# A linear-attention block feeding a sparse causal-attention block: one recorded order for all instructions, PSUM in four pairs of banks

## The chip, the core and the metric

The kernel runs on one core of a Trainium2 chip. Five engines work at the same time, each through its own queue in the order in which its instructions were recorded: PE (matrix products), DVE (vector work), ACT (functions and copies), POOL (vector work that doesn't touch PSUM) and SP, which issues the transfers. The metric is the time of one launch on the device in microseconds (us). The three runs of the kernel before took 366.65, 371.04 and 371.76 us, a median of 371.04 us.

## The reference, cut to what matters

The input has 4 batches, 4 heads, 1088 tokens and 32 numbers per head. The first block squares two small projections of each key and query and runs attention without a softmax over them. The second block routes each token of the 128-wide result to 2 of 4 experts, each of which is a causal softmax attention over all 1088 tokens.

```python
phi(x): a = S1 @ x; b = S2 @ x            # 8 numbers each; all 64 products a_i*b_j
kv = sum over tokens of phi(k) * v;  z = sum of phi(k)
x  = (phi(q) @ kv) / (phi(q) @ z + 1e-6)  # 4 heads side by side: 128 numbers a token
logits = x @ w_gate;  the 2 best of 4 experts get softmax weights w
for each expert e:  scores = (x wq[e]) (x wk[e])^T / 8, causal
                    ye = softmax(scores) @ (x wv[e]) @ wo[e]
out = sum over the two chosen experts of w * ye
```

## The kernel before, in words

Both kernels fold `wq` and `wk` of an expert into one 128x128 matrix (`Mq`) and `wv` and `wo` into another (`Mo`). So the keys of every expert are the transposed activations `xT`, its values are `x` itself, and only the queries differ. A token has two slots, one for each chosen expert. A tile is 64 tokens with two slots: 128 rows. A batch has 17 tiles in three groups of 6, 6 and 5.

The work on a batch, with the lines of the profile:

- **Preparation** (`prepare`): load and transpose k and q; sketch them by small products (L478), copy the sketches out, multiply them to 64 features (L498); sum the features times v (L532, "sums"); transpose the query features (L546); multiply them by the sums (L567, `numer`); divide (L575 to L578); transpose to `xT` (L584); store `x` to memory and fetch it back in another layout (`xr`, tiles xra to xrc).
- **The choice**: gate logits (L628), comparisons on DVE (L649 to L659), weights of the two experts on POOL (L690 to L711). The masks of who chose whom go through memory to all partitions (L667, L671), as one byte per token.
- **Queries** of a group (L751): four products with `Mq`, two copied by ACT (L770) and all four picked by mask on DVE (L761, `copy_predicated`) into `qs`.
- **Scores** of a tile (L793) in chunks of at most 512 keys, one PSUM bank each. DVE takes a chunk out with the causal mask and a running minimum (L798), ACT exponentiates (L813), DVE inverts the sum (L818), POOL scales (L822), DVE transposes into `AT` (L827).
- **Values** of a group ("the V block", L847): products of 32 rows each, over all keys up to the group's end, into four banks. ACT and DVE read the sums out and mask them (L869, L879, L883), and POOL multiplies the outer two experts' part by their masks (L876).
- **Outputs** of a group (L903): four products with `Mo` for each 128 tokens, a copy (L911), stores (L917).

Eight PSUM banks: four single ones for everything that passes (`bank`), and a tile `V` of four banks, of which each group's V block takes one of two column ranges. During the first batch's preparation the four banks of `V` serve that work.

The order is made by the class `Plan`: each job has an engine, a length in us, a rank and the results and buffers that it needs. `Plan.order` plays the jobs against these lengths and takes, for each engine, the ready job of the lowest rank. The result is recorded once; on the chip each engine runs its list strictly in that order. Work on the next batch's preparation is ranked among the scores of this one, so that the small products of L478, L567, L584 and L628 stand between the large ones.

## Time and profile before

| | |
|---|---|
| median of three runs | 371.04 us |
| profiled execution, first to last instruction | 372.6 us |
| PE busy | 311.7 us (84%) |
| DVE busy | 209.0 us (56%) |
| ACT, POOL busy | 139.1 and 140.0 us |
| chain of waits that ended last | PE 53%, DVE 17%, POOL 9%, ACT 9%, issue 9% |
| moved by DMA | 24.37 MB |

The profiled execution has no time of its own beside the span; its 372.6 us stand 1.6 us above the median of the runs. Busy PE means that a product was somewhere in its pipeline, so 100% doesn't say that the array worked at its best rate. A stretch's granted clock of 1.00 is 2.4 GHz and 0.50 is 1.2 GHz; the column shows 1.00 before the first recorded change at 62 us, and there the lengths of the products have to be read. A wait is named after what released it last.

### The profile page before, as it was taken

What the parts mean: (1) busy time and instruction counts of PE and PEld (TensorE: products, weight loads), DVE (VectorE), ACT (ScalarE), POOL (GpSimd) and SP (SyncE); (2) the same over time, 40 slices, a digit from 0 to 9 for tenths busy, and PEclk for the clock granted to TensorE, in tenths of its full rate; (3) what the DMA queues carried; (4) which work ended last, traced back from release to release, by engine and by line L of the source; (5) the groups of instructions that cost most, each with busy time, mean ns of one, the idle gap of its engine ahead of it and who ended that gap; (6) DMA issues with size and microseconds to landing.
All of it is one profiled execution on the core that took longest, in us unless ns stands there. A gap on an engine that the chain in (4) does not pass through costs nothing.

```text
span 372.6 us, 11200 instructions
## 1 busy us (share of the span) xinstructions
PE 311.7 (84%) x4662; PEld 235.4 (63%) x4662; DVE 209.0 (56%) x611; ACT 139.1 (37%) x401; POOL 140.0 (38%) x236
## 2 busy tenths in 40 slices
PE   0876785799999689999996899899968999976953
PEld 0864642386658559866585598585746965846853
DVE  4540244636787671567976604659694279573330
ACT  1013233346452252564532525644424057162210
POOL 5100345445224626663246166542362044322220
PEclk9999998559999899999998999899987999996996
DMA  8931498374100307640103177001003390000000
GB/s 180 163 60 18 76 175 157 75 117 66 41 26 21 90 23 143 117 65 19 49 19 83 33 135 125 27 2 42 21 19 95 78 172 13 2 21 3 2 19 21
DMA packets 79038, 24.37 MB, mean 65 GB/s; under 512 B 51084, under 2 KB 77964, under 8 KB 78988
## 3 DMA queue, kind: packets, MB, share of 16 engines
q1 hardware_dynamic: 78972, 23.66, 32.4%
q8 instruction: 36, 0.59, 0.7%
q14 instruction: 14, 0.11, 0.1%
q10 hardware_dynamic: 16, 0.00, 0.0%
HBM read 19.18 MB, written 4.48 MB: 63 GB/s over the span
## 4 chain that ended last, share of the span: by engine, by line
PE 53%; DVE 17%; POOL 9%; ACT 9%; issue 9%; DMA 2%; SPq 0%; DVEq 0%; POOLq 0%; ACTq 0%
PE V L847 15%; PE bank L793 10%; PE bank L903 10%; DVE A L798 3%; POOL fp L498 3%; ACT A L813 3%; DVE AT L827 3%; PE V L478 2%; PE bank L532 2%; PE bank L751 2%; PE bank L567 2%; DVE agg L879 2%; POOL A L822 1%; DVE agg L883 1%; PE V L546 1%
## 5 line engine op out<-in xcount | busy, mean ns | idle before, releaser
L822 POOL TENSOR_SCALAR A<-A,rs,sh 128x192 f32<-128x192 f32 (+16 forms) x68 | 55.5, 821 | 97.7 <-DVE rs L818 92.4
L793 PE MATMUL bank<-xT,qs 128*128 128x320 f32 (+11 forms) x216 | 83.2, 507 | 4.5 <-DVE qs L761 2.5
L813 ACT ACTIVATE A<-A,mx 128x192 f32<-128x192 f32 (+16 forms) x68 | 52.4, 771 | 55.6 <-DVE mx L798 54.6
L827 DVE STREAM_TRANSPOSE AT<-A 128x192 f32<-128x192 f32 (+16 forms) x68 | 51.9, 768 | 15.8 <-POOL A L822 15.4
L793 PEld LDWEIGHTS bank<-xT,qs 128*128 128x128 f32 x216 | 38.5, 201 | 29.2 <-issue 9.3
L903 PE MATMUL bank<-Mo,agg 128*128 128x128 f32 (+1 forms) x288 | 43.2, 314 | 13.9 <-POOL g L703 8.7
L847 PE MATMUL V<-AT,xra 32*128 32x192 f32 (+5 forms) x1152 | 48.2, 316 | 6.0 <-DVE AT L827 6.0
L847 PEld LDWEIGHTS V<-AT,xra 32*128 32x128 f32 x1152 | 43.7, 195 | 14.2 <-DVE AT L827 9.7
L903 PEld LDWEIGHTS bank<-Mo,agg 128*128 128x128 f32 (+1 forms) x288 | 39.9, 217 | 19.8 <-POOL g L703 10.5
L751 PE MATMUL bank<-xT,Mq 128*128 128x384 f32 (+1 forms) x96 | 39.0, 529 | 4.8 <-DVE qs L761 4.0
L876 POOL TENSOR_TENSOR agg<-agg,uw 128x384 f32<-128x384 f32 (+1 forms) x24 | 22.4, 954 | 50.4 <-ACT uw L869 48.1
L798 DVE CUSTOM_DVE_ANT_0 A<-bank,mask 128x320 f32<-128x320 f32 (+11 forms) x68 | 33.9, 509 | 11.9 <-PE bank L793 11.4
L879 DVE TENSOR_TENSOR agg<-V,mb 128x384 f32<-128x384 f32 (+1 forms) x24 | 12.2, 529 | 44.6 <-PE V L847 37.5
L869 ACT COPY uw<-V 128x384 f32<-128x384 f32 (+1 forms) x24 | 9.9, 464 | 60.6 <-DVE agg L879 45.9
L751 PEld LDWEIGHTS bank<-xT,Mq 128*128 128x128 f32 x96 | 18.4, 208 | 19.2 <-DVE qs L761 8.1
L798 DVE CUSTOM_DVE_ANT_0 A<-bank,mask,mx 128x320 f32<-128x320 f32 (+7 forms) x40 | 23.9, 608 | 10.3 <-PE bank L793 8.5
L847 PE MATMUL V<-AT,xrb 32*128 32x160 f32 (+5 forms) x768 | 27.2, 290 | 0.0
L847 PEld LDWEIGHTS V<-AT,xrb 32*128 32x128 f32 x768 | 25.8, 185 | 1.3 <-issue 1.1
L761 DVE COPY_PREDICATED qs<-mb,bank 128x384 f32<-128x384 uint8 (+1 forms) x48 | 23.8, 545 | 2.4 <-ACT qs L770 1.7
L492 POOL TENSOR_TENSOR kab<-kab 128x256 f32<-128x256 f32 (+1 forms) x6 | 4.8, 793 | 43.1 <-ACT kab L488 43.1
L818 DVE RECIPROCAL rs<-rs 128x1 f32<-128x1 f32 x68 | 10.1, 153 | 19.0 <-ACT rs L815 18.5
L815 ACT ACTIVATE rs<-zs 128x1 f32<-128x1 f32 x68 | 13.8, 203 | 2.1
(134 smaller groups left out, 374.4 us busy)
## 6 DMA issues: line engine op xcount, KB each, us to landing
xra<-xd SPq DMA_DIRECT2D x16, 192.0 KB
xrb<-xd SPq DMA_DIRECT2D x16, 192.0 KB
xrc<-xd SPq DMA_DIRECT2D x16, 160.0 KB
qin<-in_q_dram SPq DMA_DIRECT2D x16, 136.0 KB
mb<-md SPq DMA_DIRECT2D x7, 288.0 KB
kin<-in_k_dram SPq DMA_DIRECT2D x12, 136.0 KB
vp<-in_v_dram SPq DMA_DIRECT2D x12, 128.0 KB
xd<-xs SPq DMA_DIRECT2D x8, 192.0 KB
```

Source lines behind the costliest of these rows:

```text
L751: nc.tensor.matmul(plan[t][:, 0:w].rearrange("p (h t s) -> p h t s", h=2, s=32), Mq[:, e], xv, start=True, stop=True)
L761: nc.vector.copy_predicated(mine(l), halves(plan[mb][:, c, 0:w]), halves(plan[t][:, 0:w]))
L793: nc.tensor.matmul(plan[p][:, 0 : c1 - c0], plan[qs][:, 128 * t : 128 * t + 128], plan[xT][:, c0:c1], start=True, stop=True)
L798: nc.vector.tensor_tensor_reduce(out=plan[A][:, c0:c1], in0=plan[p][:, 0:w], in1=msk, scale=-1.0, scalar=mx[:, b, i, x - 1 : x] if x else ...
L813: nc.scalar.activation(out=a, in_=a, func=ACTF.Exp, bias=mx[:, b, i, last : last + 1], scale=-1.0, accum_out=zs[:, b, i : i + 1])
L815: nc.scalar.add(rs[:, b, i : i + 1], zs[:, b, i : i + 1], 1e-9)
L822: nc.gpsimd.tensor_scalar(out=a, in0=a, scalar1=rs[:, b, i : i + 1], scalar2=plan[("sh", b)][:, i : i + 1], op0=ALU.mult, op1=ALU.mult)
L827: nc.vector.transpose(dst[:, 0 : keys // 32, t], plan[A][:, 0:keys].rearrange("p (j s) -> p j s", s=32))
L847: nc.tensor.matmul(plan[Vk][:, g, lo : 32 * nt], plan[(f"xr{j // 12}", b)][rows, j % 12], a[rows, j, lo:], start=(j == 0), stop=(j == J - 1))
L876: nc.gpsimd.tensor_tensor(out=a, in0=a, in1=plan[uw][:, x, 0:w], op=ALU.mult)
L879: nc.vector.tensor_tensor(out=halves(plan[agg][:, 1 + x, 0:w]), in0=part(x), in1=halves(plan[mb][:, 1 + x, 0:w]), op=ALU.mult)
L903: nc.tensor.matmul(plan[p][0:m, 128 * x : 128 * x + 128], plan[agg][:, e, 128 * x : 128 * x + m], Mo[:, e], start=(e == 0), stop=(e == E - 1))
```

## The change

**One recorded order.** `Plan` no longer plays anything. `ORDER` is a list of 1283 job numbers, and `run` records the jobs in it; a letter b picks the second of two engines where a job may run on either, or drops a job that may be dropped. Forty jobs of two products on a cleared tile are offered ahead of the first real work; eight are kept, all of them before the first sketch.

**PSUM as four pairs of banks.** Every user takes a pair: two chunks of scores side by side, two experts' queries, 8 transposes, 6 tiles of `numer`. A V block holds two pairs and gives them back. There is no private `V`.

**Fused takes and picks.** DVE takes a tile's two chunks out in one instruction (72 takes instead of 108), and picks two experts in one `copy_predicated` (24 instead of 48, each twice as long).

**Natural token order, bf16 masks.** Tokens of a group stay in order instead of being split into halves, so that each group's output leaves in one or two stores (16 in all instead of 48) and the masks of a batch in two stores (8 instead of 22). Masks are bf16; they are read as 16-bit integers by the picks, and POOL multiplies by them directly: twice two experts at once (24 instructions, each twice as long). The V sums of the inner experts are now copied (ACT or DVE) and not multiplied on DVE; ACT's widening of masks is gone.

**Whole-array sketches.** After the first batch a tile of 128 tokens is sketched by one 128x128 product (9 instead of 36 small ones). `numer` uses one 128x128 product with a block-diagonal right side of 66 columns (18 instead of 72 of 33 columns) in all batches.

The jobs keep their names for lines that now stand elsewhere: sketches L475 and L487, sums L549, feature transposes L567, `numer` L590, x transposes L605, logits L660, queries L803, scores L841, V block L913, outputs L963; on DVE takes L853, picks L816, choice L686 to L697, inverting L880, transposes into `AT` L889, V patches L936 and copies L189.

**Where the order moves work, 1.** PE after the V block of the first batch's second group (`AT` are transposed softmax weights, `xrb` rows of `x`, `agg` the masked sums that the outputs read). Before, outputs follow four score products of the last tile:

```order
L847 MATMUL V<-AT_98,xrb_84 128x64 x8
L847 MATMUL V<-AT_98,xrb_84 128x32 x8
L793 MATMUL bank_66<-xT_81,qs_96 128x512
L793 MATMUL bank_67<-xT_81,qs_96 128x512
L793 MATMUL bank_65<-xT_81,qs_96 128x384
L793 MATMUL bank_64<-xT_81,qs_96 128x384
L903 MATMUL bank_66<-Mo,agg_105 128x128 x12
L793 MATMUL bank_65<-xT_81,qs_96 128x320
```

Now, after the same V block:

```order
L913 MATMUL pair_63<-AT_96,xrb_85 128x32 x2
L913 MATMUL pair_66<-AT_96,xrb_85 128x32 x2
L803 MATMUL pair_64<-xT_83,Mq 128x384 x2
L567 MATMUL pair_65<-ident,fp_77 128x128 x8
L841 MATMUL pair_66<-xT_82,qs_95 128x384
L803 MATMUL pair_63<-xT_83,Mq 128x384 x2
```

The next batch's queries (on `xT_83`) stand directly behind the V block, and no small product stands within it. This group's own outputs come after the third group's V block.

**2.** DVE around the choice for the second batch. Before, the V sums are read behind it:

```order
L827 STREAM_TRANSPOSE AT_99<-A_101 128x30x32
L649 TENSOR_TENSOR gt<-L_86 128x68x4
L650 TENSOR_TENSOR gt<-L_86 128x68x4
L651 TENSOR_TENSOR gt<-gt,lower 128x68x4
L653 TENSOR_REDUCE rank<-gt 128x68
L655 TENSOR_SCALAR c_141<-rank 128x17x4
L657 TENSOR_TENSOR c_141<-c_141 128x17x2
L658 STREAM_TRANSPOSE cT<-c_141 64x544
L659 TENSOR_REDUCE g_144<-L_86 128x17
L879 TENSOR_TENSOR agg_105<-V,mb_90 128x384 x2
L883 COPY_PREDICATED agg_105<-mb_90,V 128x384 x2
```

Now, from the end of the choice:

```order
L697 TENSOR_REDUCE ch_87<-ch_87 128x17
L734 STREAM_TRANSPOSE cT<-c_123 64x128
L880 RECIPROCAL rs<-rs 128x1
L853 ISA w_76,mx<-pair_65,mask 128x960
L853 ISA mx 128x1
L889 STREAM_TRANSPOSE AT_97<-w_74 128x28x32
L889 STREAM_TRANSPOSE AT_97<-w_71 128x32x32
L189 COPY agg_99<-pair_66 128x2x6x32
L936 COPY_PREDICATED agg_99<-mb_91,pair_66 128x2x6x32
```

A take and two transposes now stand between the choice and the reads of the sums. The read is a copy, and of a group's four such copies ACT makes the others.

**3.** PE at the start (`SKW` holds S1 and S2, `ident` an identity, `fp` features, `kvz` the sums). Before, from the first sketch:

```order
L478 MATMUL V<-SKW,kT_71 64x32 x72
L478 MATMUL V<-SKW,qT_72 64x32 x72
L358 MATMUL V<-ident,AT_98 128x128 x4
L532 MATMUL V<-vp_70,fp_75 64x33 x36
L546 MATMUL V<-ident,fp_76 128x128 x12
L358 MATMUL V<-ident,AT_98 128x128 x2
L546 MATMUL V<-ident,fp_76 128x128 x6
L363 MATMUL V<-AT_98 128x128 x8
L567 MATMUL V<-kvz_78,fp_77 64x33 x24
```

Now, from the last of four sketches:

```order
L475 MATMUL pair_66<-SKW,in_67 64x32 x40
L341 MATMUL pair_63<-ident,AT_96 128x128 x4
L567 MATMUL pair_64<-ident,fp_78 128x128 x4
L567 MATMUL pair_65<-ident,fp_78 128x128 x4
L341 MATMUL pair_63<-ident,AT_96 128x128 x2
L549 MATMUL pair_66<-vp_70,fp_77 64x33 x36
L567 MATMUL pair_64<-ident,fp_78 128x128 x4
L567 MATMUL pair_63<-ident,fp_78 128x128 x4
L590 MATMUL pair_65<-kvz_80,fp_79 128x66 x6
L567 MATMUL pair_63<-ident,fp_78 128x128 x2
L590 MATMUL pair_66<-kvz_80,fp_79 128x66 x6
```

The weight products (L363 before, L352 now) stand ahead of `numer` before and behind all of it and the first logits now.

The diff, cut to its core:

```diff
+ORDER = """
+45 47 71 46 0 1 41a 35b 3 37a 2 48 11a 70 83 25a 84 75 73 72 51 74 53 49 52 77 18a 30a 24a 78 28a 76 85 80 86 50 92
...
+        free = {p: deque(range(len(b))) for p, b in self.pools.items()}
+        for word in order:
+            n, a = (int(word[:-1]), "ab".index(word[-1])) if word[-1] in "ab" else (int(word), 0)
+            j = self.jobs[n]
...
+            if j["eng"][a] != "-":
+                for h in j["holds"]:
+                    if h not in self.where:
+                        self.where[h] = free[h[0]].popleft()
+                j["f"](j["eng"][a])
...
-    V = pp.tile([128, 4, 512], F32, tag="V", name="V")
-    banks = [pp.tile([128, 512], F32, tag=f"bank{x}", name=f"bank{x}") for x in range(4)]
...
+        "ps": [pp.tile([128, 2, 512], F32, tag=f"pair{x}", name=f"pair{x}") for x in range(4)],
+        "in": several("in", 3, [128, 128 * NJ]),
+        "vp": several("vp", 1, [128, NJ, H, D + 1]),
+        "w": several("w", 6, [128, 128 * NJ]),
...
+        "mb": several("mb", 3, [128, 6, GW], BF16),
...
+    for x in range(40):
+        h = ("ps", "dummy", x)
+        job(f"dummy{x}", ("PE", "-"), (0.43, 0.0), lambda e, h=h: [
+            nc.tensor.matmul(plan[h][:, 0], idle[:, 0:128], idle, start=True, stop=True) for _ in range(2)],
+            ["idle"], None, [h], mode="F", rank=-190 + 0.01 * x)
...
+        def sketch_all(nm, j0, j1, t):
+            src = plan[("in", nm + "T", b)]
+            for j in range(j0, j1):
+                nc.tensor.matmul(plan[t][:, (j - j0) // 4, 128 * (j % 4) : 128 * (j % 4) + 128], src[:, 128 * j : 128 * j + 128],
+                                 SKW.rearrange("p s x h r -> p (s x h r)"), start=True, stop=True)
...
+        def numer(x0, x1, t):
             f = plan[qpT].rearrange("p (y s) -> p y s", s=128)
             for y in range(2 * x0, 2 * x1):
-                c = (D + 1) * (y - 2 * x0)
-                for x in range(2):
-                    for half in (0, 64):
-                        rows = slice(64 * x, 64 * x + 64)
-                        nc.tensor.matmul(plan[ts[x]][half : half + 64, c : c + D + 1], f[rows, y, half : half + 64],
-                                         plan[kvz][rows, y % 2], start=True, stop=True)
+                z = y - 2 * x0
+                c = 2 * (D + 1) * (z % 6)
+                nc.tensor.matmul(plan[t][:, z // 6, c : c + 2 * (D + 1)], f[:, y],
+                                 plan[kvz][:, y % 2].rearrange("p x d -> p (x d)"), start=True, stop=True)
...
+        def pick(x):
+            c = plan[mb][:, 2 - 2 * x : 4 - 2 * x].bitcast(U16)
+            nc.vector.copy_predicated(chosen(), rows(c), rows(plan[ps[x]]))
...
+            if a == 2:
+                o, msk = o.rearrange("p (a s) -> p a s", a=2), msk.rearrange("p (a s) -> p a s", a=2)
+                src = plan[p][:, :, 0 : w // 2]
+            else:
+                src = plan[p][:, 0, 0:w]
             nc.vector.tensor_tensor_reduce(
-                out=plan[A][:, c0:c1], in0=plan[p][:, 0:w], in1=msk, scale=-1.0,
+                out=o, in0=src, in1=msk, scale=-1.0,
...
+        Vk = [("ps", "V", b, n, l) for l in range(2)]
...
-        def widen(x):
-            nc.scalar.copy(plan[agg][:, 3 * x, 0:w], plan[mb][:, 3 * x, 0:w])
-
-        def outer(x):
-            a = plan[agg][:, 3 * x, 0:w]
-            nc.gpsimd.tensor_tensor(out=a, in0=a, in1=plan[uw][:, x, 0:w], op=ALU.mult)
-
-        def inner(x):
-            nc.vector.tensor_tensor(out=halves(plan[agg][:, 1 + x, 0:w]), in0=part(x),
-                                    in1=halves(plan[mb][:, 1 + x, 0:w]), op=ALU.mult)
...
+        def keep(e, x):
+            copy(e, by_half(plan[agg][:, x]), sums_of(x % 2))
 
         def patch(x):
-            nc.vector.copy_predicated(halves(plan[agg][:, 1 + x, 0:w]), halves(plan[mb][:, E + x, 0:w]), part(1 - x))
+            nc.vector.copy_predicated(by_half(plan[agg][:, 2 + x]), by_half(plan[mb][:, 4 + x].bitcast(U16)), sums_of(1 - x))
+
+        def spread_sums(x):
+            a = plan[agg][:, 2 * x : 2 * x + 2, 0:w]
+            nc.gpsimd.tensor_tensor(out=a, in0=a, in1=plan[mb][:, 2 * x : 2 * x + 2, 0:w], op=ALU.mult)
...
-        for j in order:
-            j["f"]()
+        plan.run(ORDER)
```

## Rows read from the trace of the kernel before

**Rows 1.** The page, busy time, share of the span, instructions of each engine.

```profile
PE 311.7 (84%) x4662; PEld 235.4 (63%) x4662; DVE 209.0 (56%) x611; ACT 139.1 (37%) x401; POOL 140.0 (38%) x236
```

**Rows 2.** Windows of PE: stretch, length, busy, granted clock, DMA share, GB/s.

```profile
95.00:120.00 25.00, 25.00 (x417) 1.00 0.12 33
120.00:145.00 25.00, 21.08 (x323) 0.93 0.25 64
...
195.00:220.00 25.00, 21.08 (x331) 0.93 0.27 67
...
273.00:300.00 27.00, 22.84 (x321) 0.87 0.33 80
...
325.00:340.00 15.00, 9.42 (x60) 0.82 0.05 14
...
sum 372.60, PE 311.73; mean PE 20.78
```

**Rows 3.** Windows of DVE, the same columns.

```profile
300.00:325.00 25.00, 19.91 (x57) 1.00 0.33 55
```

**Rows 4.** Timeline of PE, start to first V block: start, length, instructions, idle before.

```profile
9.09 4.26 PE L478 MATMUL V<-SKW,kT 64*64 64x32 f32 x144 [9.09 <-DVE SKW L338]
...
52.38 2.75 PE L751 MATMUL bank<-xT,Mq 128*128 128x384 f32 x4
...
55.32 0.91 PE L751 MATMUL bank<-xT,Mq 128*128 128x384 f32 x2
...
68.75 0.53 PE L793 MATMUL bank<-xT,qs 128*128 128x64 f32 x2
```

**Rows 5.** Timeline of PE, the first V block.

```profile
87.87 3.18 PE L847 MATMUL V<-AT,xra 32*128 32x192 f32 x96
```

**Rows 6.** Timeline of DVE, from the landing of S1 and S2.

```profile
5.27 0.77 DVE L311 TENSOR_SCALAR A<-A 32x32 int32<-32x32 int32 x3 [4.36 <-DMA A<-in_S_dram]
...
8.05 0.23 DVE L335 STREAM_TRANSPOSE A<-A 32x64 f32<-32x64 f32 x1
```

**Rows 7.** Timeline of PE, 95 to 170 us.

```profile
97.33 0.90 PE L567 MATMUL bank<-kvz,fp 64*64 64x33 f32 x48
...
125.42 4.48 PE L903 MATMUL bank<-Mo,agg 128*128 128x128 f32 x24 [2.91 <-POOL g L703]
...
136.22 1.37 PE L847 MATMUL V<-AT,xra 32*128 32x160 f32 x32
137.52 0.69 PE L478 MATMUL bank<-SKW,kT 64*64 64x64 f32 x32
...
141.38 3.44 PE L847 MATMUL V<-AT,xrb 32*128 32x160 f32 x96
...
151.22 2.96 PE L903 MATMUL bank<-Mo,agg 128*128 128x128 f32 x23
...
157.70 1.04 PE L546 MATMUL bank<-ident,fp 128*128 128x128 f32 x8
```

**Rows 8.** Timeline of DVE, the choice and the reads of V.

```profile
118.78 0.40 DVE L649 TENSOR_TENSOR gt<-L 128x272 f32<-128x272 f32 x1
...
122.73 1.00 DVE L879 TENSOR_TENSOR agg<-V,mb 128x384 f32<-128x384 f32 x2
...
123.66 1.02 DVE L883 COPY_PREDICATED agg<-mb,V 128x384 f32<-128x384 uint8 x2
```

**Rows 9.** Groups by line and shape: count, busy us, mean ns, idle before.

```profile
L798 DVE CUSTOM_DVE_ANT_0 A<-bank,mask 128x512 f32<-128x512 f32 x8 | 5.4, 676 | 0.6 <-PE bank L793 0.6
...
L798 DVE CUSTOM_DVE_ANT_0 A<-bank,mask 128x192 f32<-128x192 f32 x4 | 1.4, 348 | 0.0
...
L798 DVE DVE_READ_ACCUMULATOR2_ANT mx<- 128x1 f32 x108 | 8.9, 83 | 0.0
...
L876 POOL TENSOR_TENSOR agg<-agg,uw 128x384 f32<-128x384 f32 x16 | 15.6, 999 | 22.3 <-ACT uw L869 20.0 <-PE bank L546 2.4
...
L876 POOL TENSOR_TENSOR agg<-agg,uw 128x320 f32<-128x320 f32 x8 | 6.7, 864 | 28.1 <-ACT uw L869 28.1
```

1087 lines of the change are left out of this document (550 added, 537 removed).

## The prediction, on record before the result

> **What bounds the kernel now.** I read the busy times first, then the windows of PE by stage, then the timelines of PE and DVE. PE is busy 311.7 of 372.6 us, and no other engine is over 56% [rows 1]. So the time is PE's work, plus what PE waits, plus what it loses at the lower clock.
>
> The windows [rows 2] tell three kinds of stretch apart. From 95 to 120 us PE is busy all the time at 2.4 GHz, and here only less work or fewer interruptions help. From 120 to 145, 195 to 220 and 273 to 300 us, once a batch, about 4 us of idle time appear, and the granted clock falls. The rest is the start and the end. The first score product stands at 68.75 us [rows 4] and the first V block at 87.87 us [rows 5], nearly a quarter of the span, though the inputs S1 and S2 have landed at 5.27 us [rows 6]. At the end, 325 to 340 us, PE is idle 5.6 of 15 us.
>
> The clock has two levels here, seen best in the lengths. Four products of 384 columns take 2.75 us from 52.38 us on, but two take 0.91 us at 55.32 us [rows 4]: 0.64 against 0.37 us each once some 0.17 us of latency are off, so 1.2 GHz and then 2.4. A batch's first outputs after a wait of 2.91 us take 4.48 us for 24; a later set of 23 takes 2.96 us [rows 7].
>
> **The change, part by part**, as differences to the profiled 372.6 us.
>
> *The start: -17.* Before the first score the new order needs the same chain: S1 and S2 decoded, spread, k and q sketched, features, sums, `numer`, division, transposes, logits, choice, masks, queries, picks. Decoding takes 3.0 us [rows 6] and loses 5 of 21 small instructions; two transposes stand before the spreading, so the first sketch stays near 9.4 us. From there I add PE's list at the lower clock. Sketches: 4 parts, 8.7 us by [rows 4] doubled. Transposes: 33; eight take 1.04 us at the upper level [rows 7], so 0.11 each there and 0.22 below: 7.3. Sums 4.3 (72 at twice the price of the small ones). `numer`: 36 instructions with 128 columns of weights, again 0.22: 7.9. The next batch's q sketch, 18 of the same: 4.0. Weight products, logits, mask products: about 7. Six queries at 1.37: 8.2. That is 47.4 us, so 56.8 at the lower level throughout with no wait. Before, the clock was up from about 55 us; with the weight products and other waits moved behind `numer`, I let the last 12 us of work run at the upper level (-6) and add 2 of waiting: first score at 53 us, 16 earlier. From there to the first V block the old kernel took 19.1 us; takes and picks lose fixed parts, and I take 18: V block at 71, so -17. Bounds: -8 (lower level throughout, one more wait) and -27 (upper level from the first sketch). I hold nearer the middle because the only long stretch like it stayed at the lower level.
>
> *Dearer small products: +6.* A `numer` third of 48 small instructions takes 0.90 us [rows 7], so 2.5 us a batch after latency. The new form is 36 instructions with 128x128 weights and 66 columns. By columns alone they would cost 2.0 us, by the transposes' 0.11 us (same weights, 128 columns) 3.9. I take 3.9, since the weights are the same: +1.4 for each of three later batches. A sketch is 18 such instructions, 2.0 us against 1.5 (two parts like the 0.69 of 32 instructions [rows 7], the second of 40); four come after the first V block: +2. Bounds: -1 and +8.
>
> The Trainium skill, TensorEngine Tiling (Array Packing), section Theoretical Speedup, speaks against this part: a product with 64 or fewer rows or columns gains up to twice by using tiles of the array. By that page `numer`, half of whose right side is now zeros, would double to 5.0 us (an estimate from the page), and the sum would be 3 us higher. No run here shows it yet; the trace has a 128x128 price only for other lines.
>
> *Fewer changes of tile shape: -8.* In the instruction lists PE goes from one tile shape (rows by columns of the array) to another 86 times after the first V block before, and 40 times now. A chunk of 32 V products between sketches takes 1.37 us; 96 in one piece take 3.44 [rows 7]. Three chunks would be 4.11, so 0.67 for two more breaks, 0.17 per change: 46 x 0.17. Bounds: 0 and -10.
>
> *The stall behind the choice: -16.* After V's end DVE runs the choice for the next batch from 118.78 us on and reads the V sums only at 122.73 and 123.66 us [rows 8]; PE's outputs start at 125.42 [rows 7]. The row names POOL's weights as the last releaser, but the patches of V ended at 124.7, so DVE's queue held it. In the new order PE has the next batch's queries and scores behind the V block, and the outputs much later. The idle 3.9, 3.9 and 4.2 us of three batches [rows 2] go: -12, and with them the lower clock after it (4.48 against 3.1 for 24 [rows 7]), 1.4 us each: -4. Late next: those queries need the picks' masks only through DVE, which is free there. Bounds: -5 and -16.
>
> *The V block needs two of four pairs: +6.* It had banks of its own. Now the last reader of each of its pairs must finish first, mostly a DVE take just ahead of it. A take of 512 columns is 0.68 + 0.08 us [rows 9]. If half of it is exposed at each of 12 blocks, that is 0.5 x 12. Bounds: 0 and +46 (below).
>
> *The end: -4.* In 325 to 340 us PE waits 5.6 us; now scores and outputs of two groups stand there, and I take 4 of it. The last V block's sums are then masked by two POOL instructions of 768 columns; from 999 ns at 384 and 864 at 320 [rows 9] that is 1.81 us each, +1.7 over before. One store instead of four gives about 1.3 us of issuing back. Bounds: -8 and +2.
>
> *At nothing.* DVE loses 36 takes' fixed part of 0.23 us (0.15 from the slope of the two shapes, 0.08 for the accumulator [rows 9]), 8.4 us, and 12 V reads; POOL gains about 20 us on 24 multiplications. Both lie beside PE's work. If that cover is gone, a V block's masking delays only outputs, placed a whole group later. The 46 transfers fewer shorten SP's queue; the late ones there are mask fetches, needed by picks several us on. bf16 masks double the bytes of one fetch, in a queue that is idle from 95 to 120 us (DMA share 0.12 [rows 2]).
>
> Sum: 372.6 - 17 + 6 - 8 - 16 + 6 - 4 = 339.6 for the profiled execution. Its span stood 1.6 us over the median of the runs, so I forecast **338 us**.
>
> **Rivals.**
>
> *The pairs stall the V blocks: 384 us, slower.* If DVE lags behind PE so that each V block waits as long as the outputs did (2.9 us) and then runs at the lower clock (1.4 us), 12 blocks cost 52 us in place of my 6. It decides once the lag at a block reaches about 2.9 us. For it: takes stand within one or two instructions of nearly every V block. Against it: in PE's fullest stretches DVE was busy at most 19.9 of 25 us [rows 3], so it can catch up. Chance 0.09.
>
> *DVE sets the pace in places: 354 us.* Between the second batch's first two V blocks I count by the rows about 18 us of DVE work (6 takes, 5 transposes, 2 picks, the choice, V's reads) beside 19 of PE's. At the 0.80 that DVE reached [rows 3] this stretch lasts 22.5, and with four stretches alike that is 16 us more. For it: little slack in a list that can't adapt. Against: takes are fused. Chance 0.17.
>
> *The order doesn't remove the waits: 368 us.* The old order was fixed as well once recorded; if jobs stand in the wrong order for the chip's real lengths, the stall behind the choice and the end's gain are replaced by others (+20) and half of the start's is lost (+8). Chance 0.11.
>
> *Everything fits: 318 us.* The dummies raise the clock before the first sketch and it holds (-9), V blocks don't wait (-6), and some of the rest of PE's 60.9 us of idle time (372.6 less 311.7 [rows 1]) goes too (-5). Against it: PE worked from 9 us on and was still at the lower level at 52 [rows 4]. Chance 0.13.
>
> **Numbers.** My forecast has the other 0.50, with its own range of 326 to 350. The range 316 to 362 takes in this, the 354 and most of the 318; the 368 and 384 are left out. Faster by over 2% means under 363.6, about what runs that spread from 366.65 to 371.76 can tell apart: 0.50 + 0.17 + 0.13 = 0.80. Within 2%: 0.11. Slower: 0.09.
>
> **What the new profile would show.** First V block near 71 us, first score near 53; the lengths of the transposes and `numer` before it tell the clock. No idle of 3 us before outputs in the middle batches. `numer` at about 0.11 us an instruction. V blocks in one piece of about 3.2, 6.8 and 9 us; before them a wait of about half a us on DVE. If DVE is over 0.85 busy for 25 us at a time while PE waits on takes, the second rival is right; if V blocks wait 3 us each, the first is. A start as long as before with the same middle would put me near 355, and show that I misread the clock.

## The result, and the profile after

The changed kernel takes 299.77 us, the median of 4 runs (298.81 to 303.18), against 369.19 us (366.65 to 371.76) in the same comparison: a ratio of 0.820 [0.811, 0.828]. The forecast was 338 us with a range from 316 to 362. The sign was right; the time lies 16 us below the range. Runs of the kernel before fall into two groups, near 367 and near 372 us, and its profiled execution is of the longer one, so the spans below differ by more (74.3 us) than the medians (69.4).

Busy times and granted clock on the page after, which answer to [rows 1]:

```profile
PE 282.3 (95%) x3922; PEld 228.1 (76%) x3922; DVE 195.9 (66%) x518; ACT 114.7 (38%) x302; POOL 158.9 (53%) x236
...
PEclk9999999799999999989999999999999999999999
```

Its span is 298.3 us. So PE is idle for 16.0 us (298.3 less 282.3) where it was idle for 60.9: 44.9 us of the 74.3 us that the span lost are idle time. The other 29.4 us are busy time. The two parts of the span, up to the first V block and from there on, as windows of PE (stretch, length, busy, granted clock, DMA share, GB/s). Before:

```profile
0.00:87.87 87.87, 61.45 (x858) 0.88 0.64 115
87.87:372.60 284.73, 250.28 (x3806) 0.95 0.24 50
```

After, and below it the stretches that answer to [rows 2]:

```profile
0.00:56.54 56.54, 47.70 (x654) 1.00 0.82 150
56.54:298.30 241.76, 234.58 (x3272) 0.99 0.37 78
95.00:120.00 25.00, 25.00 (x431) 1.00 0.21 45
120.00:145.00 25.00, 23.16 (x222) 0.93 0.60 117
195.00:220.00 25.00, 25.00 (x270) 1.00 0.34 86
...
280.00:298.30 18.30, 14.27 (x244) 1.00 0.14 40
```

The start gave 31.3 us (87.87 to 56.54), the rest 43.0 (284.73 to 241.76). Behind the first V block PE is idle for 7.2 us in all, 4.0 of them in the last 18.3 us. PE's timeline after, from the first instruction to the second batch's first queries, answers to [rows 4, 5, 7]. The trace shows an f32 product as two instructions and a bf16 product as one, so that the 6 `numer` products of an order row stand as x12 here:

```profile
1.24 5.61 PE L238 MATMUL pair<-idle 128*128 128x512 bf16 x16 [1.24 <-DVE idle L231]
7.72 3.39 PE L475 MATMUL pair<-SKW,in 64*64 64x32 f32 x206 [0.87 <-DVE SKW L189]
...
14.73 1.04 PE L567 MATMUL pair<-ident,fp 128*128 128x128 f32 x8
...
19.07 1.45 PE L590 MATMUL pair<-kvz,fp 128*128 128x66 f32 x12
...
34.13 1.79 PE L841 MATMUL pair<-xT,qs 128*128 128x64 f32 x8
...
55.37 1.24 PE L549 MATMUL pair<-vp,fp 128*64 128x33 f32 x36 [4.04 <-POOL w L497]
56.54 4.80 PE L913 MATMUL pair<-AT,xra 32*128 32x192 f32 x96
...
80.33 4.18 PE L913 MATMUL pair<-AT,xra 32*128 32x192 f32 x96
84.33 3.08 PE L913 MATMUL pair<-AT,xrb 32*128 32x192 f32 x96
87.34 1.56 PE L803 MATMUL pair<-xT,Mq 128*128 128x384 f32 x4
...
92.73 1.05 PE L963 MATMUL pair<-Mo,agg 128*128 128x128 f32 x8
```

Eight transposes take 1.04 us at 14.73 us, the length that they had at 157.70 us in [rows 7]: PE is at 2.4 GHz there, some 40 us earlier than before. The first score starts at 34.13 us and not at 68.75. From 80.33 us on, V block, queries and outputs follow each other without a wait. PE's waits by line, with the sum, the number and the longest in us, hardly hold the V block (L913) or the outputs (L963):

```profile
PE pair L549 <- POOL w L497: 4.0, 1, 4.0
PE pair L913 <- DVE qs L816: 1.8, 1, 1.8
...
PE pair L963 <- ACT ob L189: 0.3, 1, 0.3
```

Of before, the same list has PE's waits for the choice's weights (L903), for the transposes ahead of the V block (L847) and for the picks (L751):

```profile
PE bank L903 <- POOL g L703: 8.7, 3, 2.9
PE V L847 <- DVE AT L827: 6.0, 3, 4.1
PE bank L751 <- DVE qs L761: 4.0, 4, 1.0
```

### The profile page after: what moved, and what is told of

Same layout as the page of the kernel before. It is cut to its first block, busy times and chain, and to the rows that moved or that the text cites. A ratio compares the mean times of both kernels' runs of the same rounds, so it can differ in the third digit from the quotient of the medians.

```text
span 298.3 us, 9409 instructions
## 1 busy us (share of the span) xinstructions
PE 282.3 (95%) x3922; PEld 228.1 (76%) x3922; DVE 195.9 (66%) x518; ACT 114.7 (38%) x302; POOL 158.9 (53%) x236
## 4 chain that ended last, share of the span: by engine, by line
PE 82%; DMA 6%; POOL 4%; DVE 3%; issue 2%; ACT 1%; POOLq 1%; SPq 0%; DVEq 0%; ACTq 0%
PE pair L913 27%; PE pair L841 19%; PE pair L963 9%; PE pair L803 8%; PE pair L590 5%; DMA mb<-md 4%; PE pair L487 4%; PE pair L549 3%; PE pair L567 3%; PE pair L475 2%; POOL agg L940 1%; PE pair L660 1%; DVE qs L816 1%; PE pair L605 1%; POOL w L497 1%
## 5 line engine op out<-in xcount | busy, mean ns | idle before, releaser
L884 POOL TENSOR_SCALAR w<-w,rs,sh 128x768 f32<-128x768 f32 (+14 forms) x68 | 55.5, 822 | 45.2 <-DVE rs L880 41.4
L841 PE MATMUL pair<-xT,qs 128*128 128x384 f32 (+11 forms) x216 | 72.8, 475 | 1.2 <-DVE qs L816 1.2
L869 ACT ACTIVATE w<-w,mx 128x64 f32<-128x64 f32 (+14 forms) x68 | 52.4, 770 | 35.5 <-DVE mx L853 24.0
L853 DVE CUSTOM_DVE_ANT_0 w<-pair,mask 128x192 f32<-128x192 f32 (+15 forms) x68 | 48.7, 728 | 17.2 <-PE pair L841 15.4
L940 POOL TENSOR_TENSOR agg<-agg,mb 128x768 f32<-128x768 f32 (+1 forms) x24 | 37.4, 1565 | 37.9 <-ACT agg L189 26.0
L889 DVE STREAM_TRANSPOSE AT<-w 128x320 f32<-128x320 f32 (+15 forms) x68 | 50.6, 763 | 10.5 <-POOL w L884 10.3
L841 PEld LDWEIGHTS pair<-xT,qs 128*128 128x128 f32 x216 | 38.1, 190 | 23.9 <-issue 11.2
L913 PEld LDWEIGHTS pair<-AT,xra 32*128 32x128 f32 x1152 | 44.8, 198 | 7.1 <-issue 3.5
L913 PE MATMUL pair<-AT,xra 32*128 32x192 f32 (+5 forms) x1152 | 47.8, 318 | 1.9 <-DVE qs L816 1.8
L189 ACT COPY agg<-pair 128x384 f32<-128x384 f32 (+1 forms) x36 | 15.4, 463 | 68.3 <-PE pair L913 56.4
L963 PEld LDWEIGHTS pair<-Mo,agg 128*128 128x128 f32 (+1 forms) x288 | 34.3, 185 | 5.0 <-issue 2.2
L963 PE MATMUL pair<-Mo,agg 128*128 128x128 f32 (+1 forms) x288 | 36.4, 277 | 0.5 <-ACT ob L189 0.3
L803 PE MATMUL pair<-xT,Mq 128*128 128x384 f32 (+1 forms) x96 | 34.5, 480 | 0.0
L816 DVE COPY_PREDICATED qs<-mb,pair 128x768 f32<-128x768 uint16 (+1 forms) x24 | 23.3, 972 | 11.0 <-DMA mb<-md 5.2
L913 PE MATMUL pair<-AT,xrb 32*128 32x160 f32 (+5 forms) x768 | 26.4, 287 | 0.0
L913 PEld LDWEIGHTS pair<-AT,xrb 32*128 32x128 f32 x768 | 26.1, 186 | 0.0
L189 DVE COPY agg<-pair 128x384 f32<-128x384 f32 (+1 forms) x12 | 6.2, 528 | 26.5 <-PE pair L913 17.5
L803 PEld LDWEIGHTS pair<-xT,Mq 128*128 128x128 f32 x96 | 16.6, 190 | 7.3 <-issue 0.8
L936 DVE COPY_PREDICATED agg<-mb,pair 128x384 f32<-128x384 uint16 (+1 forms) x24 | 12.9, 554 | 8.4 <-ACT agg L189 7.9
L590 PEld LDWEIGHTS pair<-kvz,fp 128*128 128x128 f32 x144 | 16.9, 192 | 0.8
```

The lines of the kernel that those rows point to most:

```text
L590: nc.tensor.matmul(plan[t][:, z // 6, c : c + 2 * (D + 1)], f[:, y], plan[kvz][:, y % 2].rearrange("p x d -> p (x d)"), start=True, stop=True)
L803: nc.tensor.matmul(plan[ps[x]][:, y, 0:w], Mq[:, ((1, 2), (0, 3))[x][y]], plan[xT][:, 64 * t0 : 64 * t1], start=True, stop=True)
L816: nc.vector.copy_predicated(chosen(), rows(c), rows(plan[ps[x]]))
L841: nc.tensor.matmul(plan[p][:, y, 0 : c1 - c0], plan[qs][:, 128 * t : 128 * t + 128], plan[xT][:, c0:c1], start=True, stop=True)
L853: nc.vector.tensor_tensor_reduce(out=o, in0=src, in1=msk, scale=-1.0, scalar=mx[:, b, i, x - 1 : x] if x else 3e38, op0=ALU.add, op1=ALU.m ...
L869: nc.scalar.activation(out=a, in_=a, func=ACTF.Exp, bias=mx[:, b, i, last : last + 1], scale=-1.0, accum_out=zs[:, b, i : i + 1])
```

## The experiments

Each time is a median with its lowest and highest run; each ratio is to the kernel before on the same chip, with its 95% interval. "The list" is the class that sorted the jobs of the kernel before by their lengths and ranks. "Theory A" and "B" are as the expectations name them.

**1. The old way of ordering, on the new jobs.** `e3_list` keeps the new jobs, pairs, fused instructions and dummies, and lets the list sort them.

```diff
-        for word in order:
+        self.jobs = [j for j in every if j["eng"] != "-"]
+        for j in self.order():
...
```

> The changed kernel with its jobs, PSUM pairs, fused takes and picks, bf16 masks, whole-array sketches and dummies, but ordered by the list scheduling of the kernel before (same ranks, the job lengths that the file gives, the same choice between two engines for each job). Theory A, the searched order is what took away PE's waits: idle time of PE goes from 16 us back to 40 or more, and the clock falls in places, time 330 to 350 us. Theory B, the structure (pairs, fused work, whole-array products, the dummies) is what did it and the order is a detail: time 300 to 312 us.

317.29 us (315.30 to 317.82), 0.861 [0.854, 0.869], between the ranges of the two theories. So some 52 us come from what the jobs and buffers are, and 17.5 from the fixed order. Its first V block stands at 69.18 us and the rest takes 245.7, against 56.54 and 241.8: of the 17.5 us, 12.6 lie before the first V block and 4 behind.

Three rows show where the 12.6 come from: DVE's transpose of the choice (`cT`), SP's issue of its store to memory (`md`), and the first pick that needs the masks (`mb`) fetched from there. By the list:

```profile
38.27 0.29 DVE L815 STREAM_TRANSPOSE cT<-c 64x128 bf16<-64x128 bf16 x1
44.03 1.00 SPq L819 DMA_DIRECT2D md<-cT  x2
53.28 1.01 DVE L897 COPY_PREDICATED qs<-mb,pair 128x768 f32<-128x768 uint16 x1 [5.96 <-DMA mb<-md]
```

In the changed kernel:

```profile
30.20 0.30 DVE L734 STREAM_TRANSPOSE cT<-c 64x128 bf16<-64x128 bf16 x1
30.53 1.04 SPq L738 DMA_DIRECT2D md<-cT  x2
39.37 1.01 DVE L816 COPY_PREDICATED qs<-mb,pair 128x768 f32<-128x768 uint16 x1 [2.06 <-DMA mb<-md]
```

By the list the store is issued 5.5 us after `cT` is done, behind other transfers in SP's queue, and PE is idle for 7.0 us until 0.1 us after the pick. In the fixed order it is issued at once, and the pick comes 13.9 us earlier. No run moves these stores alone.

**2. The dummies.** `e1_no_dummies` is the changed kernel without its 16 dummy products; `e2_before_dummies` puts as many ahead of the first sketch of the kernel before.

```diff
-... 41a 35b 3 37a 2 48 11a ...
+... 41b 35b 3 37b 2 48 11b ...
```

```diff
+        lead = const("lead", [128, 512], BF16)
+        nc.vector.memset(lead, 0.0)
+        for _ in range(16):
+            nc.tensor.matmul(V[:, 0], lead[:, 0:128], lead, start=True, stop=True)
```

> The changed kernel without the eight dummy jobs (16 products on a cleared tile) ahead of the first sketch; all else and the order as they are. Theory A, the dummies are what puts PE at 2.4 GHz before the first sketch: without them the sketches, transposes, sums and numer up to about 50 us run at 1.2 GHz again, some 20 of the 42 us of PE work before the first V block take twice as long, the first V block stands 12 to 20 us later than 56.5, and the time is 312 to 320 us. Theory B, the denser list of PE raises the clock by itself within a few us: the first V block moves by at most 4 us, and the time is 298 to 304 us.

> The kernel before with the same 16 products of 512 columns on a cleared bf16 tile ahead of everything on PE; its order is untouched. Theory A, the clock is raised there and holds while PE works: the products up to 54 us, which ran at 1.2 GHz, take half as long, the first V block comes 8 to 15 us earlier than 87.9, time 354 to 361 us. Theory B, the old order leaves PE idle too often (9 us before the first sketch, gaps of 1 to 2 us behind it), so the clock falls back at once: first V block within 3 us of 87.9, time 366 to 370 us.

Without them the change takes 298.54 us (298.03 to 299.80), with them 299.77: they are worth nothing. The first V block stands at 58.79 us, within 4 us of 56.54, as theory B had it. PE's timeline without them shows why:

```profile
7.72 6.59 PE L475 MATMUL pair<-SKW,in 64*64 64x32 f32 x288 [7.72 <-DVE SKW L189]
14.24 0.66 PE L341 MATMUL pair<-ident,AT 128*128 128x128 f32 x4
```

The sketches take 1.8 us longer than the 3.39 and 1.44 us with dummies, but run in one piece, where with dummies PE is idle for 1.8 us between the two. So the transposes start at 14.24 us in both, and at the upper level without any help. In the kernel before, the dummies gave 369.99 us (363.55 to 372.38) against 367.17 (366.51 to 374.86), which tells nothing apart. The profiled execution is the shortest of its four runs. There the clock was up early and the first V block stands at 79.51 us, 8.4 earlier, but it fell back between 28 and 41 us (granted 0.61), where `numer` took 1.51 us for 48 again.

**3. How many pairs, and whose.** `e12_list_three_pairs` is `e3_list` with three pairs. `e5_list_private_v` divides the four as before: two for V (in two column ranges) and the first batch, two for all the rest. There a user of one chunk occupies a pair, so it has less than the kernel before had.

```diff
-... for x in range(4)],
+... for x in range(3)],
```

```diff
-        "ps": [pp.tile([128, 2, 512], ...) for x in range(4)],
+        "ps": pairs[:2],
+        "ps0": pairs[2:],
+        "V": [[p[:, :, c : c + 192] for p in pairs[2:]] for c in (0, 256)],
```

> The list-scheduled version (317.3 us) with three pairs of PSUM banks in the one pool instead of four. Theory A, the number of banks that a transfer between engines may use at a time sets how far PE runs ahead: 330 to 350 us, between the shared four pairs (317) and the private V (367). Theory B, what the private V cost was its privacy and not the number left: 315 to 322 us.

> The list-scheduled version (317.3 us) with PSUM divided as in the kernel before: two of the four pairs hold V in two column ranges (and the first batch's preparation), the other two pairs serve all the rest. Theory A, the lack of banks is what made PE wait in the kernel before (with the V sums read first, its outputs still waited for a score bank behind DVE's burst): 20 to 35 us slower, 337 to 352 us, with PE's waits on takes and picks back. Theory B, the banks are not the limit and the shorter work on DVE is: 315 to 325 us.

Four pairs take 317.29 us, three 331.02 (329.83 to 331.55, as theory A had it), the private division 366.92 (365.72 to 370.59, beyond both theories). The last is the time of the kernel before, with all the other edits in place. PE's waits show what is short: scores (L931), `numer` (L680) and queries (L893) wait in 17 places, 12.2 us in all, for the reading accumulator of takes (`mx`), which give pairs back; in `e3_list` such waits sum up to 1.1 us. The 11.2 us of the first row are the wait for the masks again, which `e3_list` has with 7.0.

```profile
PE pair L931 <- DVE qs L906: 13.4, 2, 11.2
PE pair L931 <- DVE mx L943: 5.4, 8, 1.1
PE pair L680 <- DVE mx L943: 3.6, 4, 2.0
PE pair L893 <- DVE mx L943: 3.2, 5, 1.1
```

**4. The banks alone, in the kernel before.** `e10_before_one_pool` gives the kernel before one pool of eight single banks; a V block takes four of them and gives them back, and its sums are read bank by bank, in twice as many instructions. `e11_before_start_banks` leaves V its own tile, but the first batch's preparation uses the four single banks. The list sorts both, so the order shifts with the buffers.

```diff
-    V = pp.tile([128, 4, 512], F32, tag="V", name="V")
-    banks = [pp.tile([128, 512], ...) for x in range(4)]
+    banks = [pp.tile([128, 512], ...) for x in range(8)]
...
+        Vk = [("ps", "V", b, n, g) for g in range(4)]
```

```diff
-        ps = "ps0" if early else "ps"
+        ps = "ps"
```

> The kernel before with one part of the change alone: PSUM as one pool of eight single banks, from which everything takes what it needs and a V block four. Its rules of order, its unfused takes and picks, its masks and its small tiles stay; the V sums are read bank by bank, so that these reads are twice as many and half as long (some 0.8 us more of DVE for each block). Theory A, the private V is what bound the kernel: 320 to 340 us, with the waits before the outputs and the queries gone and the lower clock after them. Theory B, the pool counts only together with the fused work and the whole-array products: 355 to 372 us.

> The kernel before with the first batch's preparation in the four single banks instead of in four slices of the one tile V; all else as it was. In its trace PE waits after each set of four feature transposes until ACT's copy of that same set has ended (five waits of 0.68 us), though three more slices stand free: it looks as if any write to the tile waited for every read of it. Theory A, so it is: these waits go, PE's list closes up, the clock rises earlier, and the first score product stands at 45 to 60 us in place of 68.8; time 348 to 362 us. Theory B, the waits are for the data: first score within 4 us of 68.8, 364 to 372 us.

One pool: 318.02 us (315.86 to 320.34), 0.870 [0.861, 0.878], below the range of theory A. This edit, with the order that the list makes for it, gives some 50 us, though it adds instructions. The other banks for the start: 351.08 us (350.71 to 352.32), 0.961 [0.952, 0.970], all of it before the first V block (66.12 us; behind it 283.0 against 284.7). PE's timeline with one pool, from the same place as the wait of 2.91 us in [rows 7]:

```profile
86.45 4.18 PE L845 MATMUL bank<-AT,xra 32*128 32x192 f32 x96
90.46 3.08 PE L845 MATMUL bank<-AT,xrb 32*128 32x192 f32 x96
93.46 2.95 PE L790 MATMUL bank<-xT,qs 128*128 128x512 f32 x8
96.25 0.81 PE L748 MATMUL bank<-xT,Mq 128*128 128x384 f32 x2
96.90 2.84 PE L904 MATMUL bank<-Mo,agg 128*128 128x128 f32 x24
```

Outputs follow without a wait and at the upper level. The order differs here too: DVE has done the choice at 89.70 us, ahead of the V block's end (93.54), where the kernel before does it behind (part 6).

**5. What made the start long.** `e17_before_whole_tile` changes only how the kernel before declares its PSUM: V and the four single banks are slices of one tile of eight banks. Addresses, pools, jobs and order are the same; only waits that the framework records can differ. `e16_list_one_tile` and `e18_list_two_tiles` make the pairs of `e3_list` slices of one tile of eight banks, and of two tiles of four.

```diff
-    V = pp.tile([128, 4, 512], F32, tag="V", name="V")
-    banks = [pp.tile([128, 512], ...) for x in range(4)]
+    whole = pp.tile([128, 8, 512], F32, tag="whole", name="whole")
+    V = whole[:, 0:4]
+    banks = [whole[:, 4 + x] for x in range(4)]
```

```diff
+    whole = [pp.tile([128, 4, 512], ...) for x in range(2)]
-        "ps": [pp.tile([128, 2, 512], ...) for x in range(4)],
+        "ps": [whole[x // 2][:, 2 * (x % 2) : 2 * (x % 2) + 2] for x in range(4)],
```

> The kernel before with its PSUM tiles declared otherwise: V and the four single banks are slices of one tile of eight banks. Pools, jobs, their order and every address are the same; only the waits differ that are recorded between users of different slices of V. Theory A, in the kernel before a slice of V waited for the users of the other slices: first score at 45 to 60 us in place of 68.8, nothing changes behind the first V block, 348 to 360 us. Theory B, the preparation gained only by its other place among the jobs (in e11 it shared the four single banks): 365 to 372 us.

> The list-scheduled version (317.3 us) with the same four shared pairs, but declared as slices of one PSUM tile of eight banks instead of four tiles. Same pool, same list, same instructions; only what counts as the same tile differs. Theory A, a write to one slice waits for the reads of every other slice: PE stops for each copy, take and pick, 400 us or more. Theory B, only overlapping slices wait, and the private V cost by the number of banks alone: 315 to 322 us.

> The list-scheduled version (317.3 us) with its four pairs as slices of two tiles of four banks each. Theory A, users of the two pairs of one tile wait for each other: PE waits for takes and copies of the neighbouring pair, 340 to 380 us. Theory B, as with the one tile of eight banks, nothing: 314 to 319 us.

The first takes 349.40 us (348.33 to 352.29), 0.949 [0.943, 0.955]. The first V block moves from 87.87 to 68.74 us, and the rest stays (281.8 us, before 284.7). The first score comes 26 us earlier, at 42.93 us; PE then waits for 7.64 us for picks, which wait for masks. In the kernel before, PE transposes the features in sets of four, and ACT copies each out (L550):

```profile
26.05 1.11 PE L546 MATMUL V<-ident,fp 128*128 128x128 f32 x4
27.47 1.11 PE L546 MATMUL V<-ident,fp 128*128 128x128 f32 x4 [0.30 <-ACT kvz L539]
29.26 1.11 PE L546 MATMUL V<-ident,fp 128*128 128x128 f32 x4 [0.68 <-ACT fp L550]
```

```profile
28.62 0.58 ACT L550 COPY fp<-V 128x512 f32<-128x512 f32 x1 [1.21 <-PE V L546]
```

The copy of the first set, which ended at 27.16 us, starts only when the second set, in another bank, has ended at 28.58; the third set waits for a copy. So PE and ACT take turns over banks that have nothing to do with each other. With one tile of eight banks the same work stands in one piece, and at the upper level (1.53 us for 12):

```profile
18.78 1.53 PE L547 MATMUL whole<-ident,fp 128*128 128x128 f32 x12
```

```profile
19.47 1.56 ACT L551 COPY fp<-whole 128x512 f32<-128x512 f32 x3 [0.37 <-PE whole L547]
```

One tile of eight banks costs the pairs nothing: 315.06 us (313.69 to 315.80) against 317.29. Two tiles of four cost 88 us: 405.42 (404.43 to 407.96), more than theory A had. Behind its first V block PE is then idle for 64.1 us, against 12.5 in `e3_list`. So users of different slices wait for each other in tiles of four banks and not in one of eight. One of my theories had the larger tile as the worst. These waits are in the recorded program and not a property of the chip; why the tile's size decides is open.

**6. The order behind the V block.** `e4_reads_first` is the kernel before, with the two reads of V moved ahead of the choice on DVE, three times.

```diff
+    for b in range(1, B):
+        choice = next(j for j in order if j["makes"] == ("c", b, 0))
+        reads = [j for j in order if j["eng"] == "DVE" and j["holds"][:1] == (("V", b - 1, 1),)]
...
+        order = rest[:at] + reads + [choice] + rest[at:]
```

> The kernel before with one edit to its recorded order, three times: DVE reads the V sums of the second group ahead of the next batch's choice instead of behind it. The prediction's term: the three waits of 2.9 us before the outputs go, and the lower clock after them (1.4 us each) with them, 12 to 16 us, time 353 to 358 us. Rival: the outputs wait for something else that ends nearly as late (POOL's masking of the outer experts, which runs beside the weights of the choice), so 0 to 5 us, time 364 to 370 us.

Its runs take 366.16 to 374.77 us, those of the kernel before 366.51 to 374.86: no gain. Behind the first V block the profiled execution takes 284.8 us, before 284.7. The reads now start at 117.49 and 118.42 us, but the outputs wait for 3.35 us, where [rows 7] has 2.91, and then run as slowly (4.54 us for 24). DVE's timeline, and then PE's:

```profile
118.42 1.04 DVE L883 COPY_PREDICATED agg<-mb,V 128x384 f32<-128x384 uint8 x2
...
123.15 0.67 DVE L798 CUSTOM_DVE_ANT_0 A<-bank,mask 128x512 f32<-128x512 f32 x1
```

```profile
123.98 4.54 PE L903 MATMUL bank<-Mo,agg 128*128 128x128 f32 x24 [3.35 <-DVE mx L798]
```

What released them is a take, in the queue behind the choice: the four single banks were full of scores. In the kernel before, too, the first take behind the choice ends just ahead of the outputs (125.27 and 125.42 us):

```profile
125.20 0.07 DVE L798 DVE_READ_ACCUMULATOR2_ANT mx<- 128x1 f32 x1
```

So the choice held back two things in DVE's queue, the V sums and the banks, and this edit moves only one of them. `e5_list_private_v` has the whole choice ahead of the V block's end (DVE, then PE):

```profile
105.55 0.22 DVE L787 TENSOR_REDUCE ch<-ch 128x17 f32<-128x68 f32 x1
```

```profile
106.25 3.08 PE L1003 MATMUL pair<-AT,xrb 32*128 32x192 f32 x96
...
114.82 2.84 PE L1053 MATMUL pair<-Mo,agg 128*128 128x128 f32 x24
```

There V has banks of its own as before, and the outputs at this place wait for 0, 0 and 0.6 us in the three batches, where they waited for 2.9. Two more score products stand ahead of them as well, so this is the list's order for the new jobs and not the choice alone.

**7. Fused instructions, copies, small tiles.** All from `e3_list`: `e6_list_unfused` splits takes and picks again; `e8_list_act_copies` puts the copies where they were; `e7_list_small_tiles` has `numer` and the sketches in 64x64 tiles again.

```diff
-            nc.vector.copy_predicated(chosen(), rows(c), rows(plan[ps[x]]))
+            for l in range(2):
+                nc.vector.copy_predicated(chosen()[:, l], rows(c)[:, l], rows(plan[ps[x]])[:, l])
...
```

```diff
+            elif j["eng"][0] in ("ACT", "DVE"):
+                a = 0
```

```diff
-                nc.tensor.matmul(plan[t][:, z // 6, c : c + 2 * (D + 1)], f[:, y], ...)
+                for x in range(2):
+                    for half in (0, 64):
+                        rows = slice(64 * x, 64 * x + 64)
+                        nc.tensor.matmul(plan[t][half : half + 64, x, c : c + D + 1], f[rows, y, half : half + 64],
+                                         plan[kvz][rows, y % 2, x], start=True, stop=True)
...
```

> The list-scheduled version (317.3 us) with each fused take and each pick again in two instructions; DVE gets some 10 us more work. Theory A, DVE's work is hidden beside PE's, as the prediction had it: 316 to 320 us. Theory B, DVE's bursts set when PSUM comes free and so when PE may go on: 324 to 335 us, with PE's waits for takes and picks up by 5 us or more.

> The list-scheduled version (317.3 us) with the choice of engine as in the kernel before: ACT makes all copies out of PSUM but the inner experts' V sums, which DVE reads; ACT does all the small additions, DVE all the first batch's features. Theory A, the spreading of copies over two engines shortens the start (the kernel before waited there for ACT eight times by 0.3 to 0.9 us) and frees DVE behind the V blocks: 6 to 15 us slower, most of it before the first V block, 323 to 332 us. Theory B, it is a detail: 315 to 320 us.

> The list-scheduled version (317.3 us) with numer and the later sketches in 64x64 tiles of the array as before (four products in place of one). By the prediction the whole-array form costs 1.4 us a batch for numer and 0.5 a sketch, so this one is 6 us faster: 309 to 313 us. Rival, by the lengths after: numer 17.0 us against 12.6 and sketches about alike, but the small tiles bring back changes of tile shape and more copies on ACT: 315 to 320 us.

Unfused: 319.54 us (318.59 to 320.39), 2 more, with DVE 9 us busier. Copies on ACT: 316.05 (315.48 to 319.41), no difference. Small tiles: 308.64 (308.03 to 310.99), 8.7 less. The whole-array products are a loss.

**8. Small tiles in the fixed order.** `e9_small_tiles` has the last edit in the changed kernel. `e13_changed_again` is the changed kernel unedited, `e14_small_no_dummies` has neither whole-array products nor dummies, and `e15_numer_small` has only `numer` in small tiles (the last diff of part 7); these three ran on one chip.

> The changed kernel (299.8 us), order untouched, with numer and the sketches of batches 1 to 3 again as products on 64x64 tiles of the array. In the list-scheduled version the same edit took numer from 17.1 to 9.8 us and these sketches from 13.8 to 9.7, and 8.7 us off the time. Theory A, PE sets the pace and what it saves comes off: 288 to 293 us. Theory B, the fixed order was fitted to the whole-array lengths, and PE now waits for what stands next: 295 to 300 us.

> The changed kernel itself, unedited, on the same chip as the next two: 298 to 301 us by all theories.

> The changed kernel in its order, with numer and the later sketches in 64x64 tiles and without the dummies. Theory A, PE's work saved (5.9 us at the upper clock behind the first V block) comes off where no wait eats it, and the dummies do nothing: 292 to 296 us. Theory B, the fixed order gives most of it back as waits and lower clock: 296 to 299 us, within 1% of the changed kernel.

> The changed kernel with only numer in 64x64 tiles, the sketches whole. Numer was 17.0 us against 9.8 and stands close to its readers in the order. Theory A: two thirds of what both edits give, 294 to 297 us. Theory B, lost to waits: 297 to 301 us.

| | median (6 runs each) | ratio to before |
|---|---|---|
| small tiles | 296.95 (296.12 to 298.90) | 0.8125 [0.8072, 0.8177] |
| changed again | 298.12 (294.64 to 301.61) | 0.8076 [0.8037, 0.8114] |
| small, no dummies | 296.77 (294.63 to 299.38) | 0.8073 [0.8033, 0.8113] |
| only `numer` small | 294.37 (292.11 to 296.84) | 0.8008 [0.7968, 0.8049] |

`numer`, by line and shape (count, busy us, mean ns, idle before), in the changed kernel and in the last one:

```profile
L590 PE MATMUL pair<-kvz,fp 128*128 128x66 f32 x144 | 17.0, 273 | 0.0
```

```profile
L592 PE MATMUL pair<-kvz,fp 64*64 64x33 f32 x576 | 10.0, 221 | 0.0
```

PE has 7.0 us less to do, and the median falls by 3.8 (by the ratios 0.7%, some 2.5 us); the intervals still touch (0.8037 and 0.8049). It is the lowest median of all, and beats the change by about 1%, which isn't settled.

## Why the prediction was wrong

By the medians (369.19 us for the kernel before), the 69 us fall into steps. These are differences between kernels of which each has one thing more, some on other chips, so a step is good to 2 or 3 us.

| step | us |
|---|---|
| no waits between slices of V's tile (before to `e17`) | -20 |
| one pool for V and all others, and the list's order for it (`e17` to `e10`) | -31 |
| the other edits, small products in small tiles (`e10` to `e7`) | -9 |
| `numer` and later sketches over the whole array (`e7` to `e3`) | +9 |
| the fixed order (`e3` to the change) | -17.5 |

The prediction's terms add up to -17 before the first V block and to -16 behind it; the spans moved by -31.3 and -43.0.

**The failed step: "The V block needs two of four pairs: +6", with bounds from 0 to +46.** It has the wrong sign. I priced only what V loses by sharing, and nothing for what all others gain: scores, queries and outputs had four banks and now have eight while no V block runs. The sharing measured -31 us, all behind the first V block (281.8 to 251.0 us, 16.2 of it idle time of PE). Some of it stood in the prediction under the stall's name, and the order that the list makes for the pool isn't separated from the banks; but with pairs everywhere, taking two away for V alone costs 50 us. V's own price is one wait of 1.8 us in the whole trace of the change, and 1.7 us for the lower clock behind it (4.91 us for 96 instructions that take 3.18 from 201.01 us on):

```profile
131.51 4.91 PE L913 MATMUL pair<-AT,xra 32*128 32x192 f32 x96 [1.83 <-DVE qs L816]
```

The bound at 0 was an error of method, as nothing excluded a gain. The sum itself was off too: half a take is 0.38 us, so 12 blocks make 4.6 and not 6.

The Trainium skill, Perfetto Trace Analysis, section Optimization Strategy, says that "Consistent bubbles" on the engine that should be saturated can mean that there isn't enough PSUM for the next tile; its section Matmuls asks that independent matmul groups rotate through the banks. I hadn't weighed either. The runs agree: 317, 331 and 367 us for four pairs, three pairs and the private division.

**"The start: -17"** measured -31.3 (first V block 87.87 to 56.54), beyond its bound of -27. I took the lower clock as given and added PE's list up at its prices, 47.4 us. It was an effect of the gaps. PE paused for 0.3 to 1.2 us between short pieces, because slices of V's tile waited for each other. With the gaps closed by a declaration alone the transposes are at 2.4 GHz at 18.78 us, in the same order. My +2 for waiting and -6 for the clock sat on this reading. I read each gap's releaser and didn't ask whether the copy that it names had needed to be so late. The declaration gives 19.1 of the 31.3 us (87.87 to 68.74). The last 12.6 come with the fixed order, which issues the mask stores at once (part 1); the prediction had these transfers at nothing.

**"The stall behind the choice: -16"** named the right gap and the right queue, and half of what stood in it. The idle time went (PE is busy all of 195 to 220 us). The choice on DVE held back the takes that free score banks as well as the reads of V, so the reads moved alone gained nothing; where the list has the whole choice ahead of the V block's end the wait is gone, with shared banks (`e10`) and with private ones (`e5`). So the wait doesn't need shared banks to go; the choice moved alone wasn't tried. Of the 17.5 us of the fixed order only 4 lie behind the first V block; by the list (`e3_list`) an output waits for 0.65 us at most.

**"Dearer small products: +6"** was right in sign and mechanism, and 8.7 in the list's order (2.5 to 3.8 of it back in the fixed one, by `numer` alone). A batch's `numer` takes 17.0 / 4 = 4.25 us, for which I took 3.9, and 10.0 / 4 = 2.5 in small tiles, as I took. The rule that I weighed, up to twice for 64 rows or columns by TensorEngine Tiling (Array Packing), section Theoretical Speedup, of the Trainium skill, gave the better sum, +9: the trace shows 17.0 / 10.0 = 1.7.

**"Fewer changes of tile shape: -8"** wasn't tried by itself and stays open. The V blocks of the first batch's second and third group do stand in one piece, 7.1 and 9.1 us, against the 6.8 and 9 named. The first took 4.80 us and not 3.2: it stands behind the wait of 4.04 us, at a granted clock of 0.65.

**"The end: -4"** was too little. In the last 47.6 us of the span, from 325 us on before, PE was idle for 16.4 us and now is for 5.3. The waits of [rows 2] are gone; of the 4.0 us idle in the last 18.3, 3.6 follow PE's last product. `e10` still has 15.7 there and `e7` 8.6, so most of the -9 of the other edits lies here. The POOL products of 768 columns take 1.65 us each, for which I had estimated 1.81.

**"At nothing"** holds for the fused instructions (2 us) and the copies' engine. It doesn't hold for the mask fetches, "needed by picks several us on": by the list, picks and PE wait for them, in `e3_list` 5.96 and 7.0 us.

**The rivals.** The pairs don't stall the V blocks (chance 0.09), and DVE doesn't set the pace (0.17): 195.9 us busy of 298.3. "The order doesn't remove the waits" fell too. "Everything fits", at 318 us, had the right direction and the wrong reasons, since it counted on the dummies for the clock. Two of their sums are 2 us off: four stretches of 3.5 us are 14 and not 16, and 338 with 20 and 8 is 366 and not 368.

## What to carry to other kernels

When PE has the same gap again and again and a take or copy ends it, look at all that stands behind the same work in the queue of the engine that releases it, and count the banks that are not free. To move one of two late things gains nothing, and a set of banks that one user owns is paid for by all the others. When short pieces of work alternate with gaps of about 1 us, look whether a copy waits for a product in another bank; if so, try another declaration of the buffers first, since it changes nothing else. Before pricing a stretch at the lower clock, ask what makes the gaps in it. For a transfer that work waits for, compare the time at which its source is done with the time at which it is issued.

## What the runs showed that I had not expected

- Slices of a PSUM tile of four banks, declared and used as in these kernels, wait for each other; those of one tile of eight, or tiles of their own, don't: 349.4 against 369 us, and 405.4 against 317.3. This lies in the recorded waits.
- After 6.59 us of small products in one piece, from an idle engine, PE's next products run at 2.4 GHz (four transposes in 0.66 us at 14.24 us); 16 dummy products ahead of them changed the time by little more than 1 us (298.54 and 299.77).
- With the waits at the start gone, the masks set the first V block: in `e3_list` their store was issued 5.5 us after its source was done, and PE stood for 7.0 us.
